# A fourth written-out order for a pooled attention and gated FFN kernel

## The chip, the cores and the metric

The kernel runs on one core of one Trainium2 chip. A core has a matrix engine (PE, with its weight loads PEld), a vector engine (DVE), a scalar engine (ACT), a general engine (POOL), an engine that issues transfers (SP), and 16 DMA engines that all queues share. The metric is the time of one execution on the device in microseconds (us), lower being better.

## The reference

Inputs are q, k and v of 8 batches x 8 heads x 576 rows x 64, and the weights w_in (512 x 1024), conv_w (3 x 1024) and w_out (1024 x 512), all in float32.

```python
k_p = k.reshape(B, H, Sp, 8, D).mean(axis=3)      # 72 pooled rows
v_p = v.reshape(B, H, Sp, 8, D).mean(axis=3)
scores = q @ k_p^T / sqrt(D); attn = softmax(scores)
x = (attn @ v_p), heads joined                    # 8 x 576 x 512
h = max(x @ w_in, 0)
c = conv along the sequence, three taps per channel, zero padded
out = (h * sigmoid(c)) @ w_out                    # 8 x 576 x 512
```

## The kernel before, in words

The eight batches form four groups of two (g0 to g3). Work is cut into operations: a function that emits a few instructions on one engine. For every batch there are loads (POOL issues the DMAs, which cast float32 to bfloat16 on the way), the pooling of k (for batches 0 and 1 by matmuls with a mask `pm`, L381 and L391; for the other groups by three additions on DVE, `pool_pair`, L413, and then a transpose with `pick`, L419), the transposes of q (`prep_q`, L471 and L475), and the pooling of v on DVE (`prep_v`, L441, L445). Attention runs in tiles of 128 rows: scores (L516, L529), maximum (L542), subtraction (on DVE at L554 from g1 on, on PE at L562 for g0), exponential on ACT (L580), transpose of the result, product with v (L616), and division on DVE (`att_divide`, L629 and L631). From group 2 on, the transposes of the exponentials (`att_send`, L600) and of x (`att_out`, L640) are DMA transposes that SP issues; before that they are matmuls (L591, L648) with a copy (L605, L656).

The FFN of a batch computes h (L661; for batch 0 by tiles, L682), rectifies on ACT (L670), does the conv as matmuls with diagonal matrices `dw` (L743, built on DVE at L366 in two halves), applies tanh on ACT (L754), gates on DVE (L765, L768, L772) and multiplies by w_out (L780). Results are copied to `osb` by ACT or DVE (`ffn_copy`, L791) and stored by SP (L803), two DMAs a tile.

No planner runs when the kernel is built. The operations are numbered in the order in which the add calls create them. `Graph.order` walks through the tuple ORDER: entry n stands for operation n // 2, and n % 2 picks one of its engines where it may run on two (copies from PSUM may run on DVE or ACT); -1 stands for a filler matmul on blank data (L374) that only keeps PE busy. FORMS picks between ways to split PE's array for some operations, and PLACES hands each buffer and PSUM bank its slot. Each engine runs its own operations strictly in the order of this list, and waits on semaphores for what it needs. Durations and landing times given in the add calls (`{"POOL": 0.65}`, `land=(LATE, kb, RATE)`) describe the operations, and no line of this kernel reads them when the list is walked.

Buffers are reused in rings: one buffer `kk` for the pairs of k (so the load for the next group waits for the transposes of the last), four `qp`, three `v`, five `osb`. The k of a pair is 1152 KB in one DMA at L265, w_in two loads at L286 and w_out one at L294. Loads of batch 0 come in parts: two halves of k, and q as 4 and 5 of 9 row blocks.

PE's instructions are read from memory in blocks of 16 KB (256 instructions) by a queue of their own, q8 in the profile, 26 times in the run.

Of the kernel before, what the change touches and what calls it, by code (L numbers as in the profile page):

```python
# [33 lines left out]
class Graph:  # L34
# [26 lines left out]
        26, 24, 2, 6, 4, 10, 36, 16, 18, 8, 12, 38, -1, -1, -1, 14, -1, 30, 28, 92,  # L61
        34, 98, 94, 40, 101, 20, -1, 96, 32, 108, 104, 22, 110, -1, 107, 102, 54, 316, 296, 318,
        116, 112, 298, 56, 320, 114, 322, 300, 58, 118, 302, 42, 336, 304, 338, 356, 307, 358, 340, 342,
        -1, 120, 376, 122, 344, 360, 124, 347, 324, 126, 327, 378, 308, 362, 348, 310, 364, 380, 350, 184,
        64, 382, 186, 366, 48, 328, 44, 191, 60, 384, 189, 312, 330, 387, 368, 50, 192, 315, 370, 196,
        195, 332, 198, 62, 352, 372, 335, 526, 506, 355, 528, 375, 220, 508, 530, 222, 510, 532, 388, 216,
        512, 390, 546, 219, 408, 548, 486, 550, 488, 534, 552, 514, 536, 490, 517, 396, 128, 492, 414, 46,
        554, 392, 130, 410, 395, 132, 557, 134, 398, 412, 538, 400, 416, 540, 466, 418, 420, 468, 68, 402,
        74, 422, 52, 518, 424, 470, 520, 404, 66, 472, 200, 494, 406, 558, 70, 542, 497, 560, 436, 545,
        202, 498, 438, 204, 76, 228, 442, 500, 426, 231, 440, 444, 428, 446, 432, 430, 206, 448, 434, 224,  # L70
        72, 452, 211, 456, 450, 227, 208, 454, 458, 562, 474, 462, 460, 746, 213, 464, 252, 215, 477, 726,
        255, 84, 748, 574, 750, 565, 248, 728, 954, 251, 502, 956, 576, 730, 505, 88, 478, 752, 958, 582,
        732, 78, 480, 754, 579, 734, 522, 136, 757, 934, 482, 737, 566, 936, 485, 138, 914, 525, 568, 938,
        960, 916, 584, 940, 140, 918, 571, 962, 604, 587, 142, 616, 965, 144, 974, 618, 920, 976, 606, 620,
        598, 978, 608, 758, 146, 600, 980, 760, 738, 602, 922, 148, 982, 740, 925, 646, 985, 150, 762, 648,
        742, 0, 926, 652, 744, 610, 928, 765, 966, 612, 968, 986, 614, 942, 650, 988, 945, 656, 232, 766,
        628, 658, 662, 990, 768, 630, 993, 640, 770, 632, 946, 642, 234, 772, 930, 634, 644, 236, 774, 948,
        933, 686, 636, 777, 688, 238, 638, 778, 690, 82, 247, 241, 970, 780, 245, 622, 973, 950, 624, 654,
        243, 953, 782, 676, 80, 626, 784, 1130, 678, 1038, 1132, 682, 1162, 1040, 1134, 692, 86, 1026, 1164, 1136,
        1062, 660, 1042, 1028, 1138, 1166, 1064, 1030, 680, 666, 684, 1066, 580, 1146, 1068, 668, 1148, 672, 1056, 1150,  # L80
        1070, 1058, 664, 1050, 1060, 706, 1052, 1072, 264, 1032, 1054, 590, 1168, 708, 1044, 266, 694, 1046, 670, 1034,
        710, 1048, 592, 268, 1036, 674, 1084, 697, 595, 256, 152, 1086, 596, 270, 1090, 786, 154, 712, 572, 156,
        1114, 158, 259, 788, 274, 1116, 802, 791, 1118, 1152, 1140, 804, 273, 1142, 277, 279, 714, 806, 284, 1144,
        717, 1094, 1088, 287, 1092, 794, 1170, 1100, 160, 698, 1096, 588, 796, 700, 280, 1154, 799, 260, 282, 1104,
        263, 162, 810, 1098, 1102, 1110, 1106, 718, 812, 720, 1074, 164, 166, 1178, 818, 1076, 1108, 1180, 1080, 722,
        1120, 1182, 1354, 702, 725, 820, 1122, 704, 1184, 1356, 856, 815, 1156, 1358, 823, 858, 1158, 850, 860, 844,
        1360, 1172, 1338, 1174, 1186, 852, 846, 854, 1340, 862, 1176, 848, 1124, 1342, 864, 1126, 288, 1160, 866, 292,
        290, 894, 295, 1078, 1362, 1112, 1188, 900, 826, 896, 800, 1190, 1370, 838, 1372, 808, 832, 840, 1374, 828,
        1192, 842, 1082, 834, 830, 884, 836, 1128, 898, 868, 902, 886, 1364, 890, 870, 1376, 888, 874, 1366, 872,
        168, 904, 1368, 876, 892, 880, 1570, 910, 792, 1258, 906, 1264, 1572, 1344, 1260, 1574, 90, 1276, 1346, 1262,  # L90
        1266, 170, 908, 1278, 878, 1268, 1378, 1246, 882, 1280, 1322, 1248, 1252, 824, 1324, 1250, 1270, 1326, 1348, 1254,
        1350, 1234, 1256, 1272, 912, 1352, 1236, 1274, 1240, 1238, 1380, 816, 1576, 1242, 1382, 1522, 1328, 1194, 172, 1244,
        1384, 1524, 1506, 994, 1526, 1330, 1196, 1508, 1528, 1312, 1510, 1530, 1512, 1714, 996, 1716, 1314, 1578, 1318, 1718,
        1018, 999, 1199, 1332, 1000, 1210, 1334, 1020, 174, 1336, 176, 1538, 1010, 1540, 1218, 1542, 1554, 178, 1212, 1544,
        1556, 1720, 1424, 1558, 1722, 1012, 1316, 1560, 180, 1532, 182, 1215, 1426, 1534, 1023, 1220, 1428, 1282, 1015, 1222,
        1292, 1224, 1284, 1580, 1294, 1546, 1288, 1442, 1582, 1298, 1418, 1514, 1320, 1454, 1420, 1536, 1444, 1422, 1286, 1456,
        1290, 1460, 1200, 1458, 1448, 1446, 1462, 1296, 1584, 1300, 1450, 1464, 1302, 1452, 1016, 1496, 1304, 1308, 1002, 1306,
        1498, 1310, 1502, 1516, 1724, 1004, 1518, 1562, 1726, 1402, 1007, 1500, 1548, 1008, 1404, 1550, 1728, 1466, 1406, 1486,
        1472, 1024, 1468, 1226, 1488, 1408, 1492, 1730, 1490, 1564, 1732, 1202, 1216, 1566, 1430, 1520, 1228, 1734, 1504, 1436,
        1552, 1746, 1204, 1470, 1748, 1568, 1432, 1207, 1438, 1750, 1434, 1386, 1230, 1440, 1762, 1476, 1764, 1410, 1478, 1766,  # L100
        1482, 1480, 1668, 1768, 1484, 1412, 1752, 1770, 1670, 1415, 1474, 1626, 1672, 1650, 1736, 1632, 1494, 1388, 1738, 1634,
        1391, 1652, 1208, 1636, 1644, 1628, 1392, 1646, 1630, 1656, 1654, 1754, 1394, 1648, 1740, 1232, 1586, 1742, 1396, 1744,
        1588, 1399, 1658, 1590, 1674, 1660, 1592, 1694, 1680, 1416, 1602, 1696, 1700, 1400, 1662, 1676, 1756, 1678, 1772, 1758,
        1618, 1774, 1760, 1638, 1664, 1698, 1682, 1620, 1666, 1776, 1640, 1622, 1604, 1642, 1624, 1704, 1607, 1684, 1608, 1706,
        1710, 1840, 1690, 1846, 1686, 1852, 1688, 1834, 1708, 1692, 1854, 1836, 1856, 1842, 1702, 1838, 1810, 1844, 1848, 1812,
        1712, 1850, 1816, 1814, 1828, 1818, 1822, 1820, 1830, 1824, 1832, 1878, 1826, 1868, 1884, 1880, 1778, 1874, 1882, 1886,
        1870, 1610, 1780, 1802, 1783, 1612, 1804, 1614, 1872, 1888, 1807, 1876, 1858, 1808, 1894, 1594, 1860, 1616, 1890, 1786,
        1864, 1892, 1784, 1862, 1866, 1794, 1596, 1896, 1796, 1599, 1788, 1600, 1799, 1914, 1791, 1922, 1792, 1916, 1800, 1906,
        1918, 1924, 1920, 1908, 1927, 1898, 1928, 1910, 1930, 1912, 1900, 1933, 1936, 1938, 1902, 1934, 1904, 1940, 1944, 1942,
    )  # L110
    FORMS = (
        1, 0, 0, 0, 0, 1, 1, 1, 1, 0, 0, 1, 0, 0, 1, 0, 0, 0, 0, 0, 0, 1, 1, 0, 0, 0, 1, 0, 1, 0, 1, 0, 1, 0, 1, 1, 1, 1, 0, 0,
        1, 1, 0, 0, 0, 0, 0, 1, 0, 0, 0, 0, 1,
    )
    PLACES = (
        0, 1, 2, 1, 0, 2, 0, 0, 1, 3, 0, 2, 0, 3, 4, 5, 0, 0, 0, 2, 1, 1, 0, 5, 6, 1, 1, 0, 0, 2, 2, 0, 2, 4, 1, 3, 0, 2, 0, 0,
        4, 2, 1, 3, 2, 0, 1, 6, 0, 2, 1, 0, 4, 0, 1, 6, 1, 2, 0, 2, 1, 2, 1, 3, 2, 4, 3, 6, 1, 0, 0, 0, 2, 0, 4, 5, 0, 1, 5, 6,
        0, 0, 2, 2, 2, 0, 4, 0, 2, 1, 0, 1, 1, 6, 0, 1, 4, 0, 2, 2, 2, 2, 3, 0, 0, 2, 4, 1, 5, 1, 4, 1, 2, 6, 1, 3, 0, 0, 3, 4,
        0, 2, 2, 0, 2, 0, 2, 2, 3, 0, 1, 1, 4, 6, 0, 1, 0, 2, 0, 1, 0, 0, 2, 4, 6, 2, 3, 2, 0, 4, 0, 4, 6, 0, 2, 2, 0, 1, 2, 6,
        7, 0, 2, 0, 4, 3, 0, 1, 4, 1, 5, 1, 1, 7, 0, 0, 2, 2, 0, 0, 6, 0, 1, 2, 0, 1, 2, 6, 3, 0, 4, 1, 0, 5, 2, 2, 0, 1, 1, 3,  # L120
        7, 1, 4, 0, 2, 0, 2, 1, 1, 0, 0, 2, 1, 2, 2, 4, 6, 1, 3, 0, 0, 2, 4, 2, 1, 2, 3, 6, 1, 7, 2, 2, 0, 4, 3, 4, 3, 6, 7, 2,
        0, 1, 0, 0, 4, 1, 1, 2, 2, 6, 0, 2, 0, 4, 0, 1, 2, 0, 4, 6, 0, 1, 4, 0, 0, 3, 2, 6, 3, 1, 0, 4, 1, 5, 2, 0, 2, 0, 1, 0,
# [44 lines left out]
def kernel(  # L167
# [657 lines left out]
    def token(ring, *key, n=1):  # L825
# [6 lines left out]
              for b, (g, i) in where.items()}  # L832

    START = -2 * SLOTS
    LATE = 1.8
    RATE, RATE_FIRST = 400e3, 285e3
    seq = [START]

# [33 lines left out]
    def first(name):  # L872
        return START - 40 + early.index(name) + nudge("l", name)
# [303 lines left out]
```

## Time and profile before

| | us |
|---|---|
| Time before, median of 3 runs | 234.96 (232.94 to 236.25) |
| The profiled execution | 236.91 |
| its span, first to last instruction | 235.1 |

| engine | busy us | share of the span |
|---|---|---|
| PE | 214.9 | 91% |
| DVE | 174.9 | 74% |
| ACT | 146.6 | 62% |
| POOL | 27.8 | 12% |

A line of the timeline has the start, the busy length, engine, source line, operation, tiles written and read, and in brackets the idle time before it with what ended it. A line of the chain has start, length and what it was spent on. A line of the stage table has the stage, its length, busy time with the number of instructions for PE, PEld, DVE, ACT and POOL, the granted clock of PE, the mean busy share of the DMA engines, and GB/s. Matmuls overlap and their ends are modelled, so a busy PE is not PE at its peak. Times differ by 1.4% between the three runs.

### The profile page before, as it was taken

The page shows a single profiled execution, that of the slowest core. Times are in us where ns is not written, and L with a number is a line of the kernel's source. Part 1 is how long each engine was busy: PE and PEld are TensorE (multiplying, and loading weights), DVE is VectorE, ACT ScalarE, POOL GpSimd, SP SyncE. Part 2 cuts the span into 40 slices and gives each one's busy share as a digit, 9 for nine tenths or more (in the row PEclk, how much of TensorE's full clock was granted, in tenths as well). Part 3 has the DMA queues.
Part 4 walks back from the last instruction along what each step waited for, and adds up shares of the span by engine and source line. Part 5 has one row for each costly group of instructions (what it writes and reads, how often), then busy time and mean ns, then how long its engine had stood idle before and what let it go on. Part 6 is the DMA issues. An engine that isn't in the chain of part 4 may idle for free.

```text
span 235.1 us, 7863 instructions
## 1 busy us (share of the span) xinstructions
PE 214.9 (91%) x3385; PEld 151.6 (64%) x3385; DVE 174.9 (74%) x369; ACT 146.6 (62%) x248; POOL 27.8 (12%) x45
## 2 busy tenths in 40 slices
PE   2798799979999999979997999999989999999991
PEld 0556689866688777646875865576646666765451
DVE  6579884999999999997899887967678225733521
ACT  2036666999988977956669474667426465675410
POOL 7930631032000600200000000000000000000000
PEclk9999999999999999999999999999999999999999
DMA  5999999999992699790464666265872786201685
GB/s 88 122 187 207 206 207 208 207 206 206 209 204 36 91 204 188 138 165 15 81 120 93 145 92 129 54 122 116 111 166 53 159 145 136 47 3 41 142 187 125
DMA packets 44166, 31.51 MB, mean 134 GB/s; under 512 B 23628, under 2 KB 39652, under 8 KB 44132
## 3 DMA queue, kind: packets, MB, share of 16 engines
q0 software_dynamic: 16288, 16.26, 43.2%
q1 hardware_dynamic: 27764, 14.70, 33.3%
q8 instruction: 26, 0.43, 0.7%
q10 hardware_dynamic: 80, 0.07, 0.1%
q14 instruction: 8, 0.07, 0.1%
HBM read 32.52 MB, written 9.44 MB: 178 GB/s over the span
## 4 chain that ended last, share of the span: by engine, by line
PE 66%; DVE 14%; DMA 5%; ACT 5%; issue 4%; POOL 2%; SPq 1%; DVEq 0%; ACTq 0%; POOLq 0%
PE psum L780 25%; PE psum L661 18%; PE psum L743 8%; PE psum L616 4%; PE psum L682 3%; DVE x L631 3%; PE psum L529 2%; DMA qp<-in_q_dram 2%; DMA xT<-x 2%; DVE gT L772 2%; ACT tg L754 2%; PE psum L591 2%; DVE kk L413 2%; DVE gT L768 2%; DVE negm L542 1%
## 5 line engine op out<-in xcount | busy, mean ns | idle before, releaser
L780 PE MATMUL psum<-w_out_sb,gT 128*128 128x512 bf16 (+1 forms) x296 | 69.4, 374 | 1.3 <-ACT osb L791 0.9
L661 PE MATMUL psum<-xT,w_in_sb 128*128 128x288 bf16 x448 | 62.8, 286 | 2.1 <-DMA xT<-x 1.2
L661 PEld LDWEIGHTS <-w_in_sb 128*128 128x128 bf16 x448 | 42.1, 97 | 15.8 <-issue 2.6
L670 ACT ACTIVATE hT<-psum 128x576 bf16<-128x576 f32 x56 | 34.4, 649 | 20.3 <-PE psum L661 20.3
L780 PEld LDWEIGHTS <-gT 128*128 128x128 bf16 x296 | 27.2, 97 | 26.5 <-issue 1.7
L754 ACT ACTIVATE tg<-psum 128x576 bf16<-128x576 f32 x64 | 37.7, 652 | 10.4 <-PE psum L743 8.3
L743 PE MATMUL psum<-hT,dw 64*64 64x288 bf16 (+4 forms) x1152 | 30.5, 246 | 2.1 <-issue 1.6
L542 DVE TENSOR_REDUCE negm<-psum 128x8 f32<-128x576 f32 (+2 forms) x37 | 27.5, 752 | 5.3 <-PE psum L516 3.1
L743 PEld LDWEIGHTS <-dw 64*64 64x64 bf16 x1152 | 25.4, 107 | 8.4 <-issue 6.9
L791 ACT COPY osb<-psum 128x512 f32<-128x512 f32 (+1 forms) x26 | 14.6, 579 | 21.8 <-PE psum L780 15.9
L631 DVE TENSOR_TENSOR x<-psum,r 128x512 bf16<-128x512 f32 (+1 forms) x37 | 25.6, 691 | 1.3
L772 DVE TENSOR_TENSOR gT<-gT,hT 128x1152 bf16<-128x1152 bf16 x32 | 24.3, 758 | 1.1
L580 ACT ACTIVATE e<-sd 128x576 bf16<-128x576 f32 x27 | 18.2, 685 | 7.3 <-DVE sd L554 6.5
L554 DVE TENSOR_TENSOR sd<-psum,negm 128x576 f32<-128x576 f32 x27 | 20.3, 755 | 0.9
L765 DVE TENSOR_SCALAR gT<-tg 128x576 bf16<-128x576 bf16 x32 | 9.4, 303 | 15.5 <-ACT tg L754 15.5
L768 DVE TENSOR_SCALAR gT<-tg 64x576 bf16<-64x576 bf16 x64 | 19.6, 307 | 1.7 <-ACT tg L754 0.5
L616 PE MATMUL psum<-vm,eT 128*128 128x130 bf16 (+5 forms) x240 | 19.0, 222 | 0.7 <-DVE vm L445 0.5
L616 PEld LDWEIGHTS <-eT 128*128 128x128 bf16 (+1 forms) x240 | 15.4, 100 | 4.5 <-issue 1.3
L629 DVE RECIPROCAL r<-psum 128x8 f32<-128x8 f32 (+1 forms) x37 | 7.5, 202 | 12.5 <-PE psum L616 12.4
L791 DVE COPY osb<-psum 128x512 f32<-128x512 f32 (+1 forms) x11 | 7.3, 665 | 11.4 <-PE psum L780 11.4
L481 ACT COPY qT<-psum 128x1152 bf16<-128x1152 bf16 (+1 forms) x11 | 11.8, 1071 | 3.0 <-PE psum L471 2.1
L441 DVE TENSOR_TENSOR v<-v 128x1280 bf16<-128x1280 bf16 (+2 forms) x24 | 13.0, 540 | 0.2
(73 smaller groups left out, 202.3 us busy)
## 6 DMA issues: line engine op xcount, KB each, us to landing
out_dram<-osb SPq DMA_DIRECT2D x70, 128.0 KB, 2.4
v<-in_v_dram POOLq DMA_DIRECT2D x8, 512.0 KB, 16.7
qp<-in_q_dram POOLq DMA_DIRECT2D x7, 576.0 KB, 17.4
kk<-in_k_dram POOLq DMA_DIRECT2D x3, 1152.0 KB, 15.9
w_in_sb<-in_moe_w_in_dram POOLq DMA_DIRECT2D x2, 512.0 KB, 17.4
w_out_sb<-in_moe_w_out_dram POOLq DMA_DIRECT2D x1, 1024.0 KB, 24.2
kk<-in_k_dram POOLq DMA_DIRECT2D x2, 288.0 KB, 4.9
kk<-in_k_dram POOLq DMA_DIRECT2D x1, 576.0 KB, 10.7
```

The source lines that it names most:

```text
L542: nc.vector.tensor_reduce(out=a["m"][0:rows], in_=a["s"][0:rows, :, 0:2 * KW].rearrange("p a (h s) -> p a h s", s=Sp), axis=AX.X, op=OP.ma ...
L554: nc.vector.tensor_tensor(out=a["d"][0:rows], in0=a["s"][0:rows, :, 0:2 * KW].rearrange("p a (h s) -> p a h s", s=Sp), in1=a["m"][0:rows]. ...
L616: nc.tensor.matmul(out=a["o"][lo:hi, h // 4, (h % 4) * (D + 1):(h % 4 + x1 - x0) * (D + 1)], lhsT=a["eT"][:, j, lo:hi], rhs=buf("vm", b)[: ...
L631: nc.vector.tensor_tensor(out=a["x"][0:rows].rearrange("p (a h d) -> p a h d", a=2, d=D), in0=ov[:, :, :, 0:D], in1=r[0:rows].unsqueeze(3) ...
L661: nc.tensor.matmul(out=banks(ps)[:, j, 0:SC], lhsT=w_in_block(dc, fb), rhs=buf("xT", g)[:, dc, i * S + j * SC:i * S + (j + 1) * SC], start ...
L670: nc.scalar.activation(out=buf("hT", b)[:, fb, :].rearrange("p (a s) -> p a s", a=2), in_=banks(ps)[:, :, 0:SC], func=ACT.Relu, scale=0.5,)
L743: nc.tensor.matmul(out=banks(pss[r ^ c])[c * D:(c + 1) * D, j, lo:hi], lhsT=dw[r * D:(r + 1) * D, tap * n_fb + fb, :], rhs=hT[r * D:(r + 1 ...
L754: nc.scalar.activation(out=tg.rearrange("p (a s) -> p a s", a=2), in_=banks(ps)[:, :, 0:SC], func=ACT.Tanh, scale=0.5,)
L768: nc.vector.tensor_scalar(out=gate[r * D:(r + 1) * D, fb], in0=tg[(1 - r) * D:(2 - r) * D], scalar1=1.0, scalar2=None, op0=OP.add)
L772: nc.vector.tensor_tensor(out=gate[:, both], in0=gate[:, both], in1=buf("hT", b)[:, both], op=OP.mult)
L780: nc.tensor.matmul(out=bank(ps)[0:rows, columns], lhsT=buf("gT", g)[:, fb, t * P:t * P + rows], rhs=w_out_sb[:, fb, columns], start=(fb == 0),
L791: copy(out=osb[0:rows, columns], in_=bank(ps)[0:rows, columns])
```

## The change

ORDER, FORMS and PLACES are replaced; the operations are the same. Some durations and landing times in the add calls change as well. What the new list does, read by engine:

- POOL: the first part of q is loaded between the two halves of k, ahead of the masks; the pool mask comes before the identity and the head mask; both halves of w_in are issued together, then v of batch 1; w_out moves ahead of v of batch 2; q5 and q7 come before the k of group 2, which came before q6, q7 and q5; v5 comes before the k of group 3; v7 is issued after about 70 us of PE's work, where it was after 102.
- PE: 15 filler matmuls instead of 7, 13 of them ahead of the first real work (4 before). Its other operations are the same in number and in split.
- DVE and ACT: the build of `pick` and of one half of `dw` move from the start to the tiles of batch 0's FFN. Of 111 copies that either engine may do, 35 are on DVE (28 before) and 76 on ACT (83 before).
- SP: stores and DMA transposes stand in another order; the first three stores now come before the first transpose, the other way round before.

```diff
     ORDER = (
-        26, 24, 2, 6, 4, 10, 36, 16, 18, 8, 12, 38, -1, -1, -1, 14, -1, 30, 28, 92,
...
+        8, 10, 2, 6, -1, -1, 14, -1, 24, -1, 4, -1, 26, -1, 12, -1, -1, -1, 34, 30,
...
     FORMS = (
...
     PLACES = (
...
-    LATE = 1.8
-    RATE, RATE_FIRST = 400e3, 285e3
+    LATE = 1.4
+    RATE, RATE_FIRST = 402e3, 402e3
...
-        o = add({"POOL": 0.65}, key, lambda: f(b, **part), uses=[toks[b]],
+        o = add({"POOL": 0.77}, key, lambda: f(b, **part), uses=[toks[b]],
...
-        lv[b] = add({"POOL": 1.25}, key, lambda: load_v(b), uses=[vtok[b]],
+        lv[b] = add({"POOL": 1.33}, key, lambda: load_v(b), uses=[vtok[b]],
...
-    win = [add({"POOL": 0.6}, first("w%d" % j), lambda j=j: load_w_in(j), land=(0.8, 2 * P * d_ff * 4, RATE)) for j in range(2)]
+    win = [add({"POOL": 0.74}, first("w%d" % j), lambda j=j: load_w_in(j), land=(LATE, 2 * P * d_ff * 4, RATE)) for j in range(2)]
...
-            o = add({"SP": 1.29}, key, lambda: att_send(g, t), after=[o, ze], uses=[e, eT], land=(2.1, 0, 1))
+            o = add({"SP": 1.29}, key, lambda: att_send(g, t), after=[o, ze], uses=[e, eT], land=(1.4, 0, 1))
```

The lines left out change other such numbers in the same way (`load_pair` 0.65 to 1.03, landing of stores 2.0 to 1.85).

## The prediction

> **What bounds the kernel now.** I read the page's busy shares first, then a table of stages that I cut where the busy engine changes.
>
> ```profile
> PE 214.9 (91%) x3385; PEld 151.6 (64%) x3385; DVE 174.9 (74%) x369; ACT 146.6 (62%) x248; POOL 27.8 (12%) x45
> ```
>
> PE looks like the bound, but its 91% is an average. The stages (window, length, then busy time of each engine, DMA share and rate) say more:
>
> ```profile
> 3.00:6.00 3.00, 1.62 (x4) 0.43 (x4) 2.22 (x10) 1.28 (x1) 2.72 (x8) 1.00 1.10 171
> 6.00:7.50 1.50, 1.50 (x19) 1.08 (x18) 1.35 (x5) 0.00 (x0) 1.50 (x3) 1.00 0.34 48
> ...
> 13.00:31.00 18.00, 15.29 (x351) 11.54 (x340) 15.15 (x30) 10.98 (x19) 5.93 (x9) 1.00 1.22 206
> 31.00:45.00 14.00, 13.97 (x277) 12.64 (x276) 10.09 (x18) 10.14 (x16) 2.52 (x4) 1.00 1.23 208
> 45.00:105.00 60.00, 56.20 (x1088) 41.80 (x1086) 57.88 (x116) 52.39 (x90) 8.22 (x11) 1.00 1.04 164
> 105.00:115.00 10.00, 9.93 (x156) 7.03 (x149) 7.15 (x15) 6.20 (x11) 0.00 (x0) 1.00 0.22 55
> 115.00:134.00 19.00, 17.36 (x324) 13.46 (x323) 17.76 (x38) 13.56 (x22) 0.00 (x0) 1.00 0.62 119
> 134.00:235.00 101.00, 95.09 (x1153) 61.02 (x1150) 58.71 (x124) 51.04 (x88) 0.00 (x0) 1.00 0.55 108
> ```
>
> DVE is the third busy time of a row: 57.88 of 60 us from 45 to 105, and 17.76 of 19 from 115 to 134. There DVE sets the pace. From 31 to 45 it is PE (13.97 of 14; DVE has 3.9 us free), and from 134 on PE again (DVE 58.71 of 101), which no order can shorten much. DMA is full (206 to 208 GB/s) from 13 to 72 us, but nearly empty from 6.0 to 7.5. So time can be won at the start, in the waits of the middle, and hardly at all behind 134 us.
>
> The single places come from the timelines, the waits and the chain:
>
> ```profile
> 4.14 1.69 POOL L306 TENSOR_SCALAR_AFFINE_SELECT pm<-pm 64x648 bf16<-64x648 bf16 x2
> 5.78 1.52 POOL L258 DMA_DIRECT2D qp<-in_q_dram  x2
> ```
> ```profile
> 13.20 1.42 DVE L542 TENSOR_REDUCE negm<-psum 128x8 bf16<-128x576 f32 x2 [0.38 <-PE psum L516]
> ```
> ```profile
> 71.41 1.27 DVE kk L413
> ...
> 124.20 4.62 DMA xT<-x
> ```
> ```profile
> 104.84 0.76 PE L743 MATMUL psum<-hT,dw 64*64 64x160 bf16 x28 [1.56 <-issue]
> ```
> ```profile
> 128.95 3.22 PE L661 MATMUL psum<-xT,w_in_sb 128*128 128x288 bf16 x25 [1.24 <-DMA xT<-x]
> ```
>
> The first q load is issued at 5.78, behind the masks, which makes the hole at 6.0 to 7.5. The first maximum starts at 13.20. The pooling of k for group 2 runs at 71.4 on the chain. PE stands still for 1.56 us in the midst of one conv group (L743), waiting for nothing but its own issue; the packets of the instruction queue q8 show a 16 KB read that begins at 102.5, together with SP's transposes of 100.2 and 102.8. At 127.7 PE waits 1.24 us for a transposed x.
>
> **The change part by part.** The numbers in the model's add calls (0.65 to 0.77, LATE, RATE) change no instruction: the order comes from the list alone, so they cost nothing. What the list changes, against the span of 235.1 (execution 236.91, 1.8 us outside the span, 1.95 above the median of 234.96):
>
> A, the start: **-1.1**. POOL now issues k, q, k, then the pool mask, then q's rest. The second q load starts after three issues (0.77 each from 1.31: 3.6) and the mask (1.69): 5.3 instead of 6.55. It landed 6.0 after issue, so 11.3 instead of 12.55. PE's list now has that part's transposes (0.54) and the scores (0.4) ahead of the first maximum: 12.2 instead of 13.20. The hole says the same: 1.5 us at 48 of 171 GB/s lose 1.1 us of transfer. Bounds: 0, if early loads are slow in themselves, and -1.5, with the slow rate of 11 to 13 us cured too. The 13 fillers ahead (0.43 to 0.47 each) end by 7.3, before q lands (2.08 + 5.1 = 7.2), so their 4 us beyond the old four lie in waiting time; without that cover each costs 0.4.
>
> B, deferred builds: **-1.0**. One half of the conv matrices (L366, 0.95 at 23.3) leaves the full stretch 20 to 25 for 31 to 45, where DVE has 3.9 us free. The pick build (0.68 at 12.4) leaves too, but stood in a wait: 0. Bounds -1.6 and 0.
>
> C, copies between ACT and DVE: **+1.3**. Seven more copies are on DVE in all. Counted by the work of PE ahead of each, those in DVE's two full stretches are eT 0.49 twice, xT 0.42, qT 0.75 three times and kT 0.46 to DVE (4.1), and kT 0.46 twice, osb 0.69, xT 0.42 and qT 0.75 away (2.8). Two more (0.49 and 0.42) fall into the free stretch. Bounds 0, if they meet DVE's waits, and +2.2. Those behind 134 us move from ACT to a DVE with 42 us free: 0.
>
> D, the stalled instruction read: **-2.0**. The conv group at 102.75 took 2.79 us against 0.78 for its like. In the new list v7's load is issued 32 us of PE work sooner (behind 70 us of it, not 102), so it has landed before the run of transposes. Bounds -2.0 and 0; I take the whole because load, store and transpose met there. The Trainium skill ("Runtime: NRT & Kernel Launch", Instruction fetch mechanics) says that crossing a 16 KB instruction block costs one tail bump, mostly hidden; by that rule D has nothing to win. The trace disagrees at this one place, by 1.56 us.
>
> E, the wait for x at 127.7: **-0.9**. The last of these transposes stands 4.8 us of PE work ahead of its matmuls, not 3.9. Bounds -1.2 and 0. Ahead of batch 7 that lead falls from 3.5 to 2.6 us, and xT lands 2.5 after issue: 0, or +0.5 if SP is late.
>
> F, k of group 2 lands later: **+1.8**. It now queues behind q5 and q7 (590 KB each at 206 GB/s: 2.9 us each), where it had stood ahead of them. Old landing: issue 48.29 + 15.9 = 64.2; new 64.2 + 5.7 - 1.1 (A) = 68.8. And three stores (262 KB each) now come near 60 to 63 us, beside these loads; in the old trace none comes before 84. How loads and stores share is shown only at 92 to 93 us, where by queue the loads moved 101 KB and the stores 182 KB:
>
> ```profile
> 92.00:93.00 1.00, 1.00 (x34) 0.57 (x34) 0.92 (x4) 1.00 (x3) 0.00 (x0) 1.00 1.18 284
> ```
>
> 786 KB at 182 take 4.3 us, in which the loads lose half of 886 KB, that is 2.2 us: landing at 71.0. DVE wants it at 71.3 - 2.1 (A, B) = 69.2, and its queue is in order: the group's maxima, gates and divides stand behind. Bounds 0 (stores fit beside: 68.8) and +3.3 (in series, 3.7 us: 72.5). The other early loads (both w_in together, w_out, v5) are wanted later than they came before: 0, as PE never waited for them.
>
> Sum: -1.1 - 1.0 + 1.3 - 2.0 - 0.9 + 1.8 = -1.9, a span of 233.2 and an execution of 235.0; on the median 233.1 (0.8% less). Two per cent (4.7 us) is about what a measurement here can tell from no change; the three runs shown lie 1.4% apart.
>
> **The rivals.** (1) *The gain passes whole*: k of group 2 is in time and the copies meet waits, C and F 0: -5.0, 230.0. For it: the lists are otherwise alike, with the same 374 matmul operations in the same tile shapes. Against it: DVE is 96% busy there. (2) *Instruction reads still stall*: D 0, 235.1. For it: PE also lost 0.91 us to issue in the transposes of q at 27.3 to 28.5, beside the q8 read of 26.2, where no DMA transpose ran; and a read comes every 256 instructions whatever the list. This is also the case that the change doesn't do what it says. The Trainium skill's rule above ends at the same time by another way. (3) *Slower: the queue of loads is late at 71 us.* If stores and loads go in series and A is nil, k of group 2 lands at 64.2 + 5.7 + 3.7 = 73.6, so DVE resumes 2.3 late instead of early; C's 1.3 comes on top, and D and E bring nothing since DVE is then the late one: +3.6, 238.6. It decides from a landing past 71.3.
>
> **How the numbers follow.** Forecast 0.45 (231.5 to 235), rival 1 0.2, rival 2 0.15, rival 3 0.2. The list is in order on five engines, so a wait that I can't see from the old trace may add some us: the range goes from 229.5, half a us below rival 1, to 238.6, rival 3. Faster by over 2% means below 230.3, about the half of rival 1 and a tail: 0.18. Slower by over 2% means above 239.7, beyond rival 3: 0.12. Within: 0.70.
>
> **What would show it.** A: first maximum near 12.2 and no hole at 6 to 7.5. B: the first w_in matmuls near 28.5 instead of 30.6. F: the pooling of k for group 2 not before 70, with a DVE wait for a DMA ahead of it. D: no conv group above 1.3 us near 100. E: no PE wait for xT near 125. C: DVE's busy time 4 us higher in all. Wrong it would be if some engine waits for a buffer or a bank that the new list hands out later, most of all ACT or SP behind 134 us, where I count nothing.

## The result, and the profile after

The changed kernel takes 232.81 us (median of 15 runs, 231.91 to 233.64) against 234.74 us for the kernel before (15 runs, 232.94 to 236.45): a ratio of 0.9907, 95% interval 0.9886 to 0.9927. That is faster by 0.9%, within the 2% that counts as no change here, and 0.3 us from the forecast of 233.1. The ratios here and below leave out executions more than 1.5% above the fastest of their kernel, and need not be the quotients of the medians.

The profiled spans lie further apart, 231.1 against 235.1. The profiled execution before (236.91) was 2.2 us above the median of its 15 runs, so the two traces show where time went, and overstate how much by about a factor of two. The page's busy shares of the kernel after:

```profile
PE 212.4 (92%) x3374; PEld 150.9 (65%) x3393; DVE 176.6 (76%) x376; ACT 143.4 (62%) x241; POOL 27.8 (12%) x45
```

DVE has 7 more instructions and ACT 7 fewer, the copies of step C. DVE's busy time rose by 1.7 us on the page, where overlapping instructions are counted once; added up one by one from the trace, its instructions take 191.4 us against 187.3, the 4 us of step C. The table of stages, cut as before (stage, length, busy time of PE, PEld, DVE, ACT and POOL, granted clock, DMA share, GB/s):

```profile
6.00:7.50 1.50, 0.69 (x3) 0.08 (x1) 1.40 (x5) 0.00 (x0) 1.43 (x5) 1.00 1.06 138
13.00:31.00 18.00, 15.02 (x348) 12.23 (x349) 15.82 (x30) 11.18 (x17) 5.39 (x8) 1.00 1.23 207
31.00:45.00 14.00, 13.59 (x295) 12.50 (x297) 11.59 (x27) 10.45 (x15) 3.38 (x5) 1.00 1.23 208
45.00:105.00 60.00, 56.38 (x1116) 42.11 (x1111) 57.31 (x115) 49.38 (x86) 7.48 (x10) 1.00 0.96 161
105.00:115.00 10.00, 8.88 (x113) 6.51 (x106) 8.31 (x17) 6.44 (x12) 0.00 (x0) 1.00 0.63 131
...
134.00:231.00 97.00, 91.35 (x1113) 58.48 (x1121) 59.09 (x124) 48.69 (x84) 0.00 (x0) 1.00 0.54 106
```

The hole at 6.0 to 7.5 us is filled (DMA share 1.06, was 0.34). From 31 to 45 DVE does 1.5 us more, the deferred build. The stage 105 to 115 is new in what it shows: PE is 1.1 us short of full there, where it had been 0.07 short. The single places, first on DVE's timeline, then in the chain, then in the waits:

```profile
12.24 1.42 DVE L544 TENSOR_REDUCE negm<-psum 128x8 bf16<-128x576 f32 x2 [0.87 <-PE psum L518]
```
```profile
51.79 19.11 DMA kk<-in_k_dram
```
```profile
DVE kk L415 <- DMA kk<-in_k_dram: 1.1, 1, 1.1
...
PE psum L618 <- ACT osb L793: 1.0, 1, 1.0
```

(Lines of the new kernel count two higher than those of the old.) The first maximum starts at 12.24. The k of group 2 lands at 51.79 + 19.11 = 70.90, and DVE waits 1.1 us for it. A wait that I did not forecast is PE's 1.0 us for a bank that an output copy (L793) has not emptied. PE's timeline at the old stalls:

```profile
29.00 1.95 PE L684 MATMUL psum<-xT,w_in_sb 128*128 128x128 bf16 x32
...
101.75 0.95 PE L745 MATMUL psum<-hT,dw 64*64 64x288 bf16 x40
...
103.94 1.03 PE L745 MATMUL psum<-hT,dw 64*64 64x288 bf16 x39
...
111.23 0.34 PE L618 MATMUL psum<-vm,eT 128*128 128x130 bf16 x3 [0.96 <-ACT osb L793]
...
128.51 0.53 PE L618 MATMUL psum<-vm,eT 128*128 128x130 bf16 x6 [0.65 <-DMA eT<-e]
```

The conv groups at 101 to 104 run at about 1 us, with no stall in their midst. No wait for xT is left near 125, but 0.65 us for an eT takes its place.

To see where the lead comes and goes, I added up PE's work from the trace (each matmul at the usual distance to the next of its shape, fillers left out) and noted when a given amount of it was done:

| PE work done (us) | before, at us | after, at us | lead |
|---|---|---|---|
| 15 | 31.5 | 28.2 | 3.3 |
| 30 | 46.2 | 44.7 | 1.5 |
| 50 | 70.0 | 67.4 | 2.6 |
| 55 | 75.7 | 74.2 | 1.5 |
| 80 | 103.5 | 102.5 | 1.0 |
| 85 | 110.3 | 107.5 | 2.8 |
| 90 | 115.3 | 113.4 | 1.9 |
| 105 | 133.6 | 130.3 | 3.3 |
| 145 | 176.0 | 171.6 | 4.4 |
| 195 | 227.5 | 223.8 | 3.7 |

The two lists do PE's work in different orders, so a row is good to about 1 us: at the 100th weight load for the conv the lead is 3.4 us (48.9 against 45.5). A lead of about 3 us is there by 28 us. The late k costs 1.1 (50 to 55), the old stall gives 1.8 (80 to 85), the wait for an output buffer takes 0.9 (85 to 90), the wait for xT gives 1.4 (90 to 105), and between 105 and 145 a wait of the old kernel for an output copy goes:

```profile
175.18 1.02 PE L780 MATMUL psum<-w_out_sb,gT 128*128 128x512 bf16 x4 [0.86 <-ACT osb L791]
```

### The profile page after: what moved, and what is told of

Its sections match the earlier page's. It is cut to its first block, busy times and chain, and to the rows that moved or that the text cites. A ratio compares the mean times of both kernels' runs of the same rounds, so it can differ in the third digit from the quotient of the medians.

```text
span 231.1 us, 7857 instructions
## 1 busy us (share of the span) xinstructions
PE 212.4 (92%) x3374; PEld 150.9 (65%) x3393; DVE 176.6 (76%) x376; ACT 143.4 (62%) x241; POOL 27.8 (12%) x45
## 4 chain that ended last, share of the span: by engine, by line
PE 46%; DMA 30%; DVE 9%; issue 4%; POOL 4%; ACT 4%; SPq 0%; POOLq 0%; ACTq 0%; DVEq 0%
PE psum L782 20%; PE psum L663 14%; DMA v<-in_v_dram 11%; DMA kk<-in_k_dram 8%; DMA w_in_sb<-in_moe_w_in_dram 7%; PE psum L745 6%; PE psum L618 3%; DMA eT<-e 3%; ACT tg L756 2%; DMA out_dram<-osb 2%; DVE gT L770 2%; DVE sd L556 2%; DVE negm L544 2%; POOL qp L260 1%; POOL kk L260 1%
## 5 line engine op out<-in xcount | busy, mean ns | idle before, releaser
L782 PE MATMUL psum<-w_out_sb,gT 128*128 128x512 bf16 (+1 forms) x278 | 67.2, 373 | 1.7 <-issue 1.0
L672 ACT ACTIVATE hT<-psum 128x576 bf16<-128x576 f32 x56 | 35.0, 649 | 23.7 <-PE psum L663 23.3
L756 ACT ACTIVATE tg<-psum 128x576 bf16<-128x576 f32 x64 | 38.2, 650 | 11.8 <-PE psum L745 6.8
L745 PE MATMUL psum<-hT,dw 64*64 64x288 bf16 (+4 forms) x1152 | 30.0, 246 | 0.9 <-ACT hT L672 0.4
L793 ACT COPY osb<-psum 128x512 f32<-128x512 f32 (+1 forms) x23 | 13.1, 578 | 19.8 <-PE psum L782 15.7
L618 PE MATMUL psum<-vm,eT 128*128 128x65 bf16 (+5 forms) x240 | 19.5, 222 | 1.9 <-ACT osb L793 1.0
L793 DVE COPY osb<-psum 128x512 f32<-128x512 f32 (+1 forms) x14 | 9.4, 669 | 11.2 <-DMA out_dram<-osb 6.6
L443 DVE TENSOR_TENSOR v<-v 128x1280 bf16<-128x1280 bf16 (+2 forms) x24 | 12.9, 538 | 2.3 <-DMA v<-in_v_dram 2.2
L531 PE MATMUL psum<-kT,qT 128*128 128x144 bf16 (+1 forms) x116 | 11.7, 227 | 1.1 <-ACT kT L434 0.7
```

Of the source, the lines that this page charges most:

```text
L618: nc.tensor.matmul(out=a["o"][lo:hi, h // 4, (h % 4) * (D + 1):(h % 4 + x1 - x0) * (D + 1)], lhsT=a["eT"][:, j, lo:hi], rhs=buf("vm", b)[: ...
L672: nc.scalar.activation(out=buf("hT", b)[:, fb, :].rearrange("p (a s) -> p a s", a=2), in_=banks(ps)[:, :, 0:SC], func=ACT.Relu, scale=0.5,)
L745: nc.tensor.matmul(out=banks(pss[r ^ c])[c * D:(c + 1) * D, j, lo:hi], lhsT=dw[r * D:(r + 1) * D, tap * n_fb + fb, :], rhs=hT[r * D:(r + 1 ...
L756: nc.scalar.activation(out=tg.rearrange("p (a s) -> p a s", a=2), in_=banks(ps)[:, :, 0:SC], func=ACT.Tanh, scale=0.5,)
L782: nc.tensor.matmul(out=bank(ps)[0:rows, columns], lhsT=buf("gT", g)[:, fb, t * P:t * P + rows], rhs=w_out_sb[:, fb, columns], start=(fb == 0),
L793: copy(out=osb[0:rows, columns], in_=bank(ps)[0:rows, columns])
```

## The experiments

Each was timed beside runs of the kernel before on the same chip, and the ratios are to those. The rounds ran on four chips, so a difference of medians from two rounds holds less than one of ratios. The changed kernel's own 0.9907 is from the result above.

### The kernel before, again, and two half lists

The first look is at the kernel before, with no edit, for how often its stall recurs. The next two take one half of the list from each kernel:

```diff
 start_new
-entries of the old list up to the first convolution of batch 0
+the new list's first 185 entries, up to that convolution
 all other operations in the old order
 start_old
 the old list's first 178 entries, up to that convolution
-all other operations in the old order
+all other operations in the new order
```

> The kernel before, profiled a second time. Theory (step D): the 2 us stall in the conv group near 102 us belongs to this order and is there again, 1 to 2 us long, with a block read beside it. Rival: that stall was an accident of the one execution that was profiled (236.9 us against a median of 234.7); then this group takes about 0.8 us and the span is near 233.

> The list of the changed kernel as far as the first conv of batch 0 (185 entries), then all that is left in the old list's order, so k of group 2 is loaded ahead of q6, q7 and q5 and the first stores stand behind 84 us, as before. Theory (A, B, and F as the price of the new loads): the start's 2.1 to 3 us come through, as nothing waits for k of group 2: 231.7 to 232.6, ratio to before 0.987 to 0.991. Rival (DVE is the bound of the middle whatever the start): the start's gain is lost in the stretch 45 to 105, ratio 0.995 to 1.

> The first 178 entries of the old list (up to the first convolution of batch 0), then the new order: the counterpart of the run with the new start and the old rest, which stayed at 0.9992 of the kernel before. Theory 1 (the rest of the list alone carries what was won, the start is given back later anyway): 0.990 to 0.994 of before, near 232.5. Theory 2 (start and rest need each other, since only together they stay ahead of the late loads): 0.997 to 1.001, near 234.2. The recorded sum without its first step of -1.1 would give 0.9955. Either way no conv group near 102 us should stall above 0.3 us, since the old rest is gone, and v7's last packet should come before 99.

The repeat of the kernel before took 236.44 us, and the stall is there again, at 0.69 us instead of 1.56. The new start alone gives 234.50, ratio 0.9992 (0.9957 to 1.0027). The new rest alone gives 235.33, ratio 1.0025 (0.9993 to 1.0057). **Neither half wins anything, and together they win 0.9%.** So the terms of a sum over such a list are not independent. The profiled execution of the new start took 238.33 us, 3.8 above the median of its runs, so it shows where that one execution lost time and not what the others do. There the lead ends on DVE, whose timeline says:

```profile
90.65 1.36 DVE L415 TENSOR_TENSOR kk<-kk 128x2304 bf16<-128x2304 bf16 x1 [3.01 <-DMA kk<-in_k_dram]
```

DVE is early for the k of group 3 and waits 3.01 us. That transfer took 14.3 us from issue to landing, where it took 9.7 in both profiles of the kernel before, and PE then waits 2.28 us for DVE at 94 us and meets the old stall as well:

```profile
106.54 0.69 PE L745 MATMUL psum<-hT,dw 64*64 64x63 bf16 x24 [0.84 <-issue]
```

With the new rest alone, PE waits for DVE and ACT 0.53, 0.74, 0.66, 0.57 and 0.42 us between 45 and 54 us, where the changed kernel waits 0.70 and 0.35. That profile took 236.22 us, 0.9 above its median.

The fourteen profiles also put step A's agreement in doubt. The first maximum starts at 11.62, 11.67, 12.75, 13.20 and 13.64 in the five with the old start (mean 12.6), and at 12.24 to 13.44 in the eight with the new start and its 13 fillers (mean 12.9). What differs comes behind it: the first weight load for w_in stands at 30.1 on the mean with the old start and at 29.3 with the new, the 128th at 39.4 and 37.6. And at the transposes of q, near 27 us, PE stands still for its own issue for 0.87 to 1.06 us in all five profiles with the old start, here in the kernel before, and in none of the nine with the new:

```profile
28.46 0.38 PE L475 MATMUL psum<-ident,qp 64*64 64x64 bf16 x24 [0.91 <-issue]
```

### The copies, put back and alone

```diff
 copies_back: the changed kernel, 21 copies ahead of 134 us
-on the engine of the new list
+on the engine of the old list, at the same places
 copies_alone: the kernel before, the same 21 copies
-on the engine of the old list
+on the engine of the new list, at the same places
```

> The changed kernel with the 21 copies ahead of 134 us that changed between ACT and DVE put back on their old engine, at the same places of the list. Theory of the recorded step C (DVE sets the pace, each copy on it costs its time): 1.3 us faster than the changed kernel, so 231.5 and 0.986 of before. Rival (the copies stand in waits of DVE, which the late k of group 2 makes anyway): the same as the changed kernel, 232.4 to 233.0. Second rival (ACT is then late for its exponentials, since its list is full at these places): 1 us slower than the changed kernel, 233.8.

> The kernel before with nothing but the engines of those 21 copies ahead of 134 us as the changed kernel has them. Putting them back cost the changed kernel 1.3 us, with 0.9 us more of TensorE's wait for kT between 45 and 60 us, where ACT is busy for 6.97 of 7 us. Theory 1 (the copies relieve ACT there, whatever the order): 1.0 to 1.5 us faster than before, 0.994 to 0.996. Theory 2 (which engine should copy is a matter of the list around it, and these were chosen for the new list): the same as before, 0.998 to 1.002. The recorded step C, a cost on DVE, would give 1.005.

Put back, they make the changed kernel slower: 234.15, ratio 0.9977 (0.9952 to 1.0002), 1.3 us above the changed kernel's 232.81 (1.6 by the two ratios). Alone in the old list they make that slower too: 236.87, ratio 1.0107 (1.0054 to 1.0161), which is 2.5 us by the ratio and 1.9 above the median of all runs of the kernel before (234.97). **The same edit costs 1.9 to 2.5 us in one list and wins 1.3 to 1.6 in the other.** The rows of the stage 45 to 52 show why the stage table had misled me; this is the kernel before, then the kernel after:

```profile
45.00:52.00 7.00, 6.01 (x177) 4.92 (x173) 6.71 (x18) 6.94 (x12) 1.82 (x2) 1.00 1.24 206
```
```profile
45.00:52.00 7.00, 5.71 (x178) 4.21 (x169) 6.75 (x17) 6.97 (x13) 0.96 (x2) 1.00 1.24 207
```

In seven of the sixty us that I had read as one stage set by DVE (57.88 of 60), ACT is busy for 6.94 of 7, more than DVE. PE's wait for a copy of kT on ACT in that stretch is 0.70 us in the changed kernel, and 1.64 with the copies put back:

```profile
49.58 0.41 PE L531 MATMUL psum<-kT,qT 128*128 128x144 bf16 x4 [0.70 <-ACT kT L434]
```
```profile
50.77 0.41 PE L531 MATMUL psum<-kT,qT 128*128 128x144 bf16 x4 [1.64 <-ACT kT L434]
```

That is 0.9 us, the largest single part of the difference. In the old list the cost comes in small steps: against the kernel before, the lead of that profile's start shrinks from 1.5 us at 15 us of PE's work to 0.1 at 95, with no single wait that I can name. Why the balance differs between the lists is not settled.

### The late k of group 2

```diff
 k2_first: POOL's part of the new list
-q5, q7, k of group 2, q6
+k of group 2, q5, q7, q6
 stores_late: SP's part of the new list
-stores of tiles 0, 1, 2 of batch 0; first transpose of group 2
+first transpose of group 2; stores of tiles 0, 1, 2 of batch 0
```

> The changed kernel, but k of group 2 is loaded ahead of q5, q7 and q6. Theory (F): it lands 5 to 6 us sooner, near 65, the DVE wait for it at 70 us goes, and 1.1 to 1.8 us of the time: 231.0 to 231.7, ratio to before 0.984 to 0.987. Rival (the wait hides in time that PE needs anyway): same as the changed kernel, 0.990 to 0.992.

> The changed kernel, but the first three stores (786 KB) stand behind the first DMA transpose of group 2, near 85 us, and not near 60. Theory (F, its share of the stores): the loads beside them are no longer slowed, k of group 2 lands 2.2 us sooner (near 68.7), and the DVE wait of about 1 us for it goes: 231.3 to 232, ratio 0.985 to 0.988. Rival: loads and stores do not hinder each other, or the stores hurt more behind 85 us, among the transposes: 0.990 or more.

With k first: 232.68, ratio 0.9934 (0.9906 to 0.9963). With the stores late: 232.06, ratio 0.9915 (0.9883 to 0.9946). The load lands at 63.10 and 68.86, from 70.90. Both take the wait for x at 72 us away (0.86 us of PE, which came from DVE's wait for k), and neither time is told apart from the changed kernel's.

PE's list is the same in these runs, so their traces can be laid beside the changed kernel's weight load by weight load (PE's weight loads are all on record there). Both win 1.0 us there between 72 and 74 us. They lose 0.2 to 0.3 of it at 111, where the wait for an output buffer is 1.13 and 1.22 us instead of 0.96. With k first another 0.6 us is lost near 52: POOL issues the load from 47.57 to 48.60, beside two gates on DVE that take 1.19 us instead of 0.62, and PE then waits for a subtraction on DVE. DVE's timeline, then PE's:

```profile
47.51 1.19 DVE L770 TENSOR_SCALAR gT<-tg 64x576 bf16<-64x576 bf16 x2
```
```profile
52.46 0.32 PE L518 MATMUL psum<-kT,qT 64*64 64x72 bf16 x16 [0.60 <-DVE sd L556]
```

So the stores do delay that load, by 2.0 us, as forecast. Of the 1.0 us that an early k wins, 0.4 is left at the end of this pair of profiles, too little for these medians to show.

### The load of v7 and the stalled instruction read

```diff
 v7_early: DVE's part of the old list
-the four steps that pool v of batch 4, near 80 us of DVE's work
+the same four steps 13 to 25 entries sooner
```

> The kernel before with one thing moved: the four preparations of v of batch 4, which free the buffer that v7's load waits for, stand some 25 entries earlier on DVE, about where the new list has them. v7's load should be issued near 92 us instead of 96.4 and its last packet come near 98 instead of 102.4 to 104.4, so ahead of the instruction read at 102 to 104. Theory D (the stall of the conv group near 103, 1.56, 0.69 and 0.84 us in the three profiles with the old rest, comes from that read meeting the end of v7's load): no stall above 0.3 us, and 0.7 to 1.5 us less than before: 0.994 to 0.997. Rival (it comes from the transposes on SP's queue that lie at the same time): the stall stays, and the time is that of before, 0.999 to 1.002. Second rival: the preparations push DVE's maxima 1.3 us later, and what goes with the stall is lost there: no stall, but 1.000.

The time is 235.25, ratio 0.9998 (0.9962 to 1.0034). The last packet of v7 comes at 99.4 instead of 102.5, and the conv group of that place on PE's timeline is whole again:

```profile
102.87 0.95 PE L743 MATMUL psum<-hT,dw 64*64 64x288 bf16 x40 [0.80 <-ACT osb L791]
```

The stall is gone, and the second rival holds: PE waits for an output copy instead (0.80), and 0.55 us for a subtraction on DVE near 92. Laid beside the kernel before, weight load by weight load, this run wins 1.8 us at the stall and loses 0.8 at each of the two places.

The stall can now be read more closely. In the four profiles that have it (the kernel before, its repeat, the new start, the copies alone) it is 1.56, 0.69, 0.84 and 1.05 us. The 16 KB read of that place begins at 102.5, 102.1, 104.3 and 102.1, each within 0.5 us of the last packet of v7 (102.5, 102.6, 104.6, 101.8), in two of them 0.3 and 0.5 us ahead of it. With v7 early it begins at 99.7, just behind v7's last packet (99.4). The read itself takes about the same or less in the four (0.95 to 1.01 us) than with v7 early (1.56). What differs is when it begins against PE's progress: where PE's list is the same, 1.8, 1.1 and 1.9 us after PE has started its first 3,328 (13 times 256) matmuls and weight loads (before, repeat, copies alone), and 0.3 to 0.5 us ahead of that with v7 early, where some matmul records are missing. In the changed kernel and the seven runs that edit it, it begins 0.1 to 0.3 us after that point. So the read starts late in the four, near the end of v7's load, and PE runs out.

In all four PE resumes 2.2 to 2.4 us after the read has begun. The five stalls at the transposes of q end at the same distance from a read, and no other wait of PE for issue in the fourteen profiles is over 0.45 us. In the changed kernel the load is over at 97.7, SP's transposes of 101.2 and 102.5 lie just ahead of the next read at 103.2, and nothing stalls: transposes beside a read do not do it by themselves. That the read waits for the load's packets is my inference. At the transposes of q the read is not shown to be late; there PE has used up its instructions 1.3 us after the read begins. Why the other reads between 20 and 70 us, beside loads too, cost little was not settled.

Three of the four stalls are from executions 1.7 us or more above the median of the kernel before (236.91, 236.44, 238.33), and only the copies alone (236.57, median 236.87) shows one in an ordinary execution, so how often the kernel before has it is not known.

The stall in the run with the copies alone:

```profile
104.41 0.75 PE L743 MATMUL psum<-hT,dw 64*64 64x160 bf16 x28 [1.05 <-issue]
```

The Trainium skill ("Runtime: NRT & Kernel Launch", Instruction fetch mechanics) has such a read cost one tail bump of a DMA that is mostly hidden. With the load out of the way the trace agrees (waits for issue of 0.16 us at most near that place in the kernel with v7 early); where the read begins late it does not, by 0.69 to 1.56 us, nor at the transposes of q in the old start, by 0.87 to 1.06.

### The fillers

```diff
 fills_four: PE's part of the new list
-13 fillers ahead of the first transpose of q
+4 fillers
```

> The changed kernel with 4 of its 13 first fillers, as the old list has them. By the recorded step A they lie in waiting time: no difference, 232.8. Rival: they set the rate of TensorE. Where the old list has 4, the 18 pooling matmuls of k took 1.29 us, and 0.73 with 13, and in three of four profiles with the new start the granted clock is 0.50 for 3 to 7 us between 11 and 18 us. With 4 fillers these matmuls should take 1.2 to 1.3 us again and the start up to the first maximum 0.5 to 1.0 us longer, of which 0 to 0.8 is left at the end: 232.8 to 233.6. The Trainium skill (TensorE: Matmul & The Clock Gate, The HAM clock gate) says that matmuls run at half the clock until about 3.4 us of sustained work have passed; by it the first preparations would be at half rate here.

232.91, ratio 0.9894 (0.9853 to 0.9935): the same as the changed kernel, as step A had it. The rate of the first matmuls does change, as the rival said. The 18 pooling matmuls on PE's timeline with 4 fillers, then with 13:

```profile
9.42 1.29 PE L381 MATMUL psum<-pm,kk 128*64 128x144 bf16 x18
```
```profile
8.32 0.73 PE L383 MATMUL psum<-pm,kk 128*64 128x144 bf16 x18
```

With 13 it is 0.73 in six of eight profiles, 1.19 and 1.29 in the others. The first maximum comes at 13.56 with 4 fillers, 0.7 us behind the mean with 13, and by 22 us this profile is 0.4 us behind the changed kernel's. The work there waits for transfers, and no difference in the time is left.

### The output buffer, and a better version

```diff
 store_up: SP's part of the new list
+store of tile 3 of batch 0
 second transpose of group 2
 ... three entries
-store of tile 3 of batch 0
 store_k2: store_up, k2_first and
-copy of kT of batch 2, first half, on ACT
+the same copy on DVE
 both_early: store_up and k2_first
```

> The changed kernel with the store of output tile 3 of batch 0 placed ahead of the second transpose of group 2 on SP's queue instead of behind four transposes: it should be issued near 93 us, when its copy is done, instead of 106. Theory (the new wait of 1.0 us at 109.9 us, where a copy waits for a buffer of the stores, costs the kernel its length): that wait goes, and the time is 0.5 to 1.0 us below the changed kernel's, 231.8 to 232.3. Rival (the order behind it makes the time up again, as with the late k of group 2): the wait goes, and the time stays at 232.5 to 233.0. Second rival (the store runs beside v7's load from 90.7 to 97.5 and makes that late): 233.5.

> The changed kernel with three edits: k of group 2 loaded ahead of q5, q7 and q6, that store moved up, and one copy of kT of batch 2 (near 48 us, where TensorE waits 0.70 us for it) moved from ACT to DVE. If each wait costs its length, 1.1 + 1.0 + 0.5 us below the changed kernel: 230.2 to 231. If the pace is set elsewhere between the waits, 232.3 to 232.8, as with each edit alone.

> The changed kernel with k of group 2 ahead of q5, q7 and q6, and the store moved up, without the third edit, after which TensorE waited 2.24 us for kT between 45 and 60 us instead of 0.70. Theory (that copy lost the third kernel 0.7 us or more, and the two early transfers each win a little): 231.0 to 231.6, 0.985 to 0.988 of before, below the store alone (0.9899). Rival (the early k wins nothing, as alone): 231.8 to 232.4, 0.990. No wait for osb between 105 and 115, and none for x between 60 and 75 us.

The store alone gives 231.85, ratio 0.9899 (0.9856 to 0.9942). The median is 1.0 us below the changed kernel's; by the ratio the two are not told apart. On SP's timeline it is issued at 93.74, where it had waited behind transposes until 106.0, and PE's wait at 111 us is gone:

```profile
93.74 1.11 SPq L805 DMA_DIRECT2D out_dram<-osb  x2
```

With all three edits it is 232.53, ratio 0.9913 (0.9880 to 0.9946). The third edit undoes the others. The copy that it moves now stands behind gates in DVE's list, and ACT, which was to be relieved, waits for it with its own copies of kT. ACT's timeline:

```profile
50.99 1.09 ACT L434 CAST kT<-psum 64x288 bf16<-64x288 f32 x3 [1.83 <-DVE kT L434]
```

PE's wait for kT in that stretch rises from 0.70 to 2.24 us, and along PE's list this run loses 1.3 us there. Without this edit, the two early transfers give **231.02, ratio 0.9817 (0.9771 to 0.9863)**, with a span of 228.9. This interval lies wholly below the changed kernel's, so it beats both kernels; whether by 2% is open.

Laid beside the changed kernel's profile from 22 us on, where the starts are done, the early k alone wins 0.4 us, the early store alone 1.1, and both together 2.1. The gain of 1.0 us at 72 to 74 and that of 1.0 to 1.2 at 111 stand whole in the run with both, and its PE doesn't wait for eT near 128 either. So the two edits about add up. That the first is worth nothing alone is not shown: its 0.4 us is less than the medians can tell.

## Why the prediction was right, and where it was not

The time was right, and partly by luck. On the scale of the two profiles the forecast was 1.9 us and the spans differ by 4.0 (235.1 to 231.1); the medians differ by 1.9, because the profiled execution before was itself 2.2 us above its median. And errors of the sum cancel. By its steps:

- **A and B, the start: -1.1 and -1.0 forecast.** On the mean of the profiles the lead at the 128th weight load for w_in is 1.8 us, near their sum of 2.1. But A's own sign, the first maximum at 12.2, agreed by luck: over all profiles it does not start sooner. The lead is made behind that, up to 31 us. The deferred builds have left DVE's list there, which would be B, but B was not tried alone, and the stall at the transposes of q, which only the old start has, is 0.87 to 1.06 us by itself. The prediction named it (0.91 us), under its second rival, and left it out of the sum. The first w_in matmuls run at 29.00, from 30.63, against 28.5 forecast. And the new start is worth nothing without the new rest.
- **C, the copies: +1.3 forecast.** The sign is wrong for this list. I priced them on DVE alone because I averaged 45 to 105 us; from 45 to 52 ACT is the fuller engine, and putting the copies back costs 1.3 to 1.6 us. For the old list the sign would have been right, and the size of 1.9 to 2.5 at or past its upper bound of 2.2.
- **D, the stall: -2.0 forecast.** The stall goes, and with v7's load moved alone it goes too. The size was taken from one profile, with a wait of 1.56 us; the mean of four is 1.04. One reason given was wrong: v7's place in POOL's list does not set its issue. In both lists POOL waits until DVE has pooled v of batch 4 and so freed the buffer, and it was these DVE steps that came sooner (issue 96.27 before, 90.74 after, 5.5 us, not the "32 us of PE work" of the text). And taking the stall away by itself gains nothing, as the early v7 shows.
- **E, the wait for xT: -0.9 forecast.** It goes, 0.65 us for eT comes, 1.24 to 0.65: -0.6.
- **F, the late k: +1.8 forecast.** The landing at 71.0 was 70.9, and the sharing of stores and loads was right (2.0 us against 2.2; the old landing was 64.4, not 64.2, as 15.9 us is the median of three loads). DVE waited 1.1 us, not 1.8: it wanted the data at 69.8, not at 69.2.
- **Not in the sum:** the new wait for an output buffer at 110 us, about +1.0, and the old wait at 174 us that went, about -0.9. "A buffer that the new list hands out later" was named as what could make it wrong, but placed behind 134 us.

Of the rivals, the first (the gain passes whole, 230.0) fails by the wait of F and the new one for the output buffer; with both removed the kernel is at 231.0. The second (reads still stall) falls for the conv group, since no profile with the new rest has that stall, and also for the transposes of q, since none with the new start has that one. The third needed a landing past 71.3; it came at 70.9. Such a landing does not make the kernel slower by itself: in the run with the early store it came at 71.55, with a time of 231.85.

The runs also spread less after the change: 1.7 us over 15, against 3.5 over 15 before. New start, new rest and early v7, each alone, still spread over 3.1 to 5.9 us. What narrows it is not settled.

## What to carry to other kernels

Before costing work moved between two engines, cut the stage until each row has one full engine: an average of 96% for DVE hid seven us in which ACT was the bound, and there the sign of the edit turned. When one wait is removed and the median doesn't move, lay the two traces beside each other along the list of the engine that sets the pace: that showed 1.0 us won by the early k, and where 0.6 of it was lost again, which medians from different chips could not. And test a place that looks right in one profile against the other profiles: the first maximum moved by 2 us between executions with the same opening.

## What the runs showed of the hardware

Between executions with the same opening instructions, the first maximum started anywhere from 11.62 to 13.64 us. The second part of q let PE go on at 9.89 to 11.37 us, and the 16 transposes behind it took 0.64 us in two of the five and 1.06 in the others.

The granted clock of PE fell to 0.50 for 3.4 or 6.8 us between 8 and 19 us in seven of the eight profiles with 13 fillers, and in one of the five with the old start (11 to 15 us), here in the stage table of the kernel with k first:

```profile
12.00:14.00 2.00, 2.00 (x40) 1.37 (x36) 1.27 (x2) 0.69 (x1) 1.34 (x2) 0.50 1.22 199
```

It did not in the one with the new start and 4 fillers. But a 1.00 near the start is no proof of the full rate: in the six profiles with 4 fillers the trace has its first entry for the clock at 7.4 to 16.9 us, and ahead of it the 18 pooling matmuls take 1.29 us in four of them, against 0.73. By the Trainium skill ("TensorE: Matmul & The Clock Gate", The HAM clock gate) the clock halves after an idle window of about 3.4 us. The trace agrees with the window's length, as the clock's changes in a start lie 3.41, 6.83 or 10.24 us apart; but PE was busy for 34 to 56% of the 3.41 us ahead of each fall, so the window need not be wholly idle. The time does not follow the clock here: the changed kernel ran a span of 231.1 us at a mean clock of 1.000, and 230.2 at 0.987.

The k of a group pair (1152 KB) landed 5.7 us after the load ahead of it when it moved alone (68.86 after 63.18, with the stores late), and 7.6 us after it with three stores beside (70.91 after 63.29, in the changed kernel).

Every gate on DVE that takes more than 0.40 us in the fourteen profiles (0.31 is usual) stands beside an issue of a load by POOL, and the longest, 0.87 us, beside that of a k of 1152 KB. Other gates beside such an issue stay short; why was not settled.
